# A new hand-written order for a fused cosine-attention and feed-forward kernel, with split first products

## The chip, the cores and the metric

The kernel runs on one core of one Trainium2 chip. The metric is the device time of one execution in microseconds (us): the median over several runs. Instruction times come from the hardware profiler's record of one execution. The engines are named as the profile names them: PE is the tensor engine, PEld its weight loads, DVE the vector engine, ACT the scalar engine, POOL the GpSimd engine and SP the engine that issues most transfers.

## The reference

Cosine attention over 8 batches of 12 heads (448 positions, 64 values each) feeds a feed-forward block with a hard-swish between its two matrices:

```python
q_n = q / (np.linalg.norm(q, axis=-1, keepdims=True) + 1e-06)
k_n = k / (np.linalg.norm(k, axis=-1, keepdims=True) + 1e-06)
scores = np.matmul(q_n, k_n.transpose(0, 1, 3, 2)) / tau
scores = scores - np.max(scores, axis=-1, keepdims=True)
attn = np.exp(scores)
attn = attn / (np.sum(attn, axis=-1, keepdims=True) + 1e-09)
attn_out = np.matmul(attn, v)
x = attn_out.transpose(0, 2, 1, 3).reshape(B * S, H * D)   # 3584 x 768
h = x @ w_in                                               # 768 x 2048
g = h * np.clip(h + 3.0, 0.0, 6.0) / 6.0
out = g @ w_out                                            # 2048 x 768
```

## The kernel before

**Work and tiling.** Heads are handled two at a time ("pairs"), one head in partitions 0 to 63 and the other in 64 to 127; there are 48 pairs, numbered 0 to 47, six to a batch. For each pair the kernel squares and sums q and k (SQ, RE), turns the sums into inverse norms (NO, four small ACT instructions), multiplies (NM), and transposes (on PE with TR for the first pairs and by a transfer, XD, later), copies the result to its place (CQ, CK, CS), multiplies keys by queries (SC), takes exponentials on ACT (EX), multiplies by the values (VA, after the values have been cast by VC), divides by the sums (FI), and turns the result around into xT (BK and CX on PE and DVE, or a transfer XB or XP).

**Feed-forward.** F.b.fc is one unit of the first product: six matmuls of 128x448 over the six 128-row parts of xT for batch b and column block fc, followed by an ACT instruction (FA) and a DVE instruction (FV) that write gT. The second product is done on pairs of 128-token tiles with seven products in place of eight (P.1 to P.7), which need sums and differences of halves of gT (G) and of w_out (WS). Their results are moved out and combined by PE.* steps on ACT or DVE, BO, RS and PL on POOL, then stored. The last two batches use the same scheme for the first product too (IS, XS, QA, QB, QC and what follows them).

**Half and whole rows.** A matmul reads 64 or 128 rows of the array. Scores of one head of a pair have an inner size of 64, so two matmuls, one on each half of the rows, run side by side; so do the values of the last, short group of keys (VA.i.3). All other matmuls use the whole 128 rows. The PE stream therefore alternates between half-row and whole-row stretches.

**Memory for results of PE.** At the start the scores go to two double banks, SC; the banks Y and Z hold transposes. OPEN closes the double banks and opens a ring of six single banks (M0, M1, Y, Z, M2, M3) that everything after it takes in turn. A bank can be taken again only when its reader is done. PV holds the values' products of one pair, so VA of the next pair waits for FI of this one.

**What sets the order.** PLAN is a hand-kept table of some 1,900 tokens. `run` performs them in turn; each token issues its instructions, and every engine executes its own in that order. A token's last letter says which engine does it, where there is a choice: v (DVE), a (ACT), p (POOL). The semaphores between engines are put in from the buffers that each instruction reads and writes. A token such as FA.0.2 or PE.3.1 performs a step that an earlier token has left behind with `post`. DP.n issues n products of zeros into an unused part of PV; their results are not read.

Of the kernel before, what the change touches and what calls it, by code (L numbers as in the profile page):

```python
# [120 lines left out]
def kernel(  # L121
# [15 lines left out]
    HP = H // 2  # L137
# [94 lines left out]
    def needs(*what):  # L232
        for w in what:
            assert w in issued or any(x < 0 for x in w[1:] if isinstance(x, int)), w
# [401 lines left out]
    def g_of(b):  # L636
        return gT[b % 2]
# [597 lines left out]
```

## Time and profile before

| | |
|---|---|
| median of 3 runs | 397.3 us (397.3 to 398.22) |
| the profiled execution | 397.24 us |
| its span, first to last instruction | 395.4 us |
| busy: PE, DVE, ACT, POOL | 97%, 78%, 75%, 75% of the span |
| products of zeros (DP) | 62 matmuls of 128x248 |

The span is 1.84 us shorter than the execution that it belongs to. [...]

### The profile page before, as it was taken

Reading aid. Unit: us, or ns where it says so; the run is one execution under the profiler, and the core shown is the slowest. Engines: PE = TensorE matmul, PEld = TensorE weight load, DVE = VectorE, ACT = ScalarE, POOL = GpSimd, SP = SyncE. Lnnn points to the kernel's source line nnn. Section 1 sums busy time; section 2 is a strip of 40 time slices with the busy share of each in tenths; the row PEclk is TensorE's granted clock in tenths of the full one; section 3 lists DMA queues with packets and bytes.
Section 4 is the critical chain, followed back from the end, with each engine's and each line's share of the span. In section 5 each row is a group of like instructions: output and inputs, shape, how many; then the busy total and the mean of one; then the engine's idle time right before and its main releaser. Section 6 shows DMA issues by size and latency. Waiting matters only on the chain.

```text
span 395.4 us, 10013 instructions
## 1 busy us (share of the span) xinstructions
PE 384.2 (97%) x3782; PEld 240.4 (61%) x3782; DVE 308.8 (78%) x545; ACT 295.3 (75%) x670; POOL 297.5 (75%) x269
## 2 busy tenths in 40 slices
PE   7898999999999999999999999999999999999995
PEld 5565556445655555655655556655566679977763
DVE  6998869988969697787767878853878968986862
ACT  6997999889966888887757876897787567744420
POOL 4999894899589947477848684778798988675752
PEclk9999999999999999999999999999999999999999
DMA  8989989798999797886995599665456350012124
GB/s 294 327 225 279 201 248 259 135 173 166 225 206 235 161 233 191 167 211 194 174 222 136 151 200 183 193 150 133 105 124 139 80 117 2 2 41 61 41 60 119
DMA packets 90239, 64.87 MB, mean 164 GB/s; under 512 B 55760, under 2 KB 89424, under 8 KB 90192
## 3 DMA queue, kind: packets, MB, share of 16 engines
q1 hardware_dynamic: 85280, 57.56, 59.1%
q0 software_dynamic: 4512, 6.29, 9.5%
q8 instruction: 29, 0.48, 0.5%
q10 hardware_dynamic: 400, 0.39, 0.3%
q14 instruction: 18, 0.15, 0.1%
HBM read 46.73 MB, written 11.01 MB: 146 GB/s over the span
## 4 chain that ended last, share of the span: by engine, by line
PE 87%; POOL 5%; DVE 2%; DMA 2%; issue 2%; ACT 1%; SPq 0%; POOLq 0%; DVEq 0%; ACTq 0%
PE M L671 18%; PE M L837 17%; PE PV L537 10%; PE V L837 6%; PE M L1026 6%; PE M L502 6%; PE Y L671 4%; PE Y L837 4%; PE Z L837 4%; PE Z L671 3%; POOL nrm L341 2%; PE Y L502 2%; PE Z L502 2%; POOL vx L363 1%; PE Y L1026 1%
## 5 line engine op out<-in xcount | busy, mean ns | idle before, releaser
L521 ACT ACTIVATE att<-M 128x448 bf16<-128x448 f32 x193 | 95.7, 561 | 13.9 <-PE M L502 12.2
L671 PE MATMUL M<-xT,w_in_sb 128*128 128x448 bf16 x396 | 82.9, 353 | 0.0
L671 PEld LDWEIGHTS <-w_in_sb 128*128 128x128 bf16 x576 | 53.1, 98 | 46.8 <-issue 3.4
L341 POOL TENSOR_TENSOR nrm<-big,r 128x896 bf16<-128x896 f32 (+1 forms) x36 | 61.7, 1720 | 15.0 <-ACT r L329 13.8
L537 PEld LDWEIGHTS <-att 128*128 128x128 bf16 (+1 forms) x1536 | 55.5, 97 | 23.0 <-issue 10.4
L537 PE MATMUL PV<-vx,att 128*128 128x65 bf16 (+1 forms) x1536 | 64.1, 193 | 0.5 <-POOL vx L363 0.5
L837 PEld LDWEIGHTS <-gT 128*128 128x128 bf16 x448 | 43.0, 98 | 27.7 <-issue 0.4
L686 DVE SCALAR_TENSOR_TENSOR gT<-u,M 128x448 bf16<-128x448 bf16 x66 | 39.5, 616 | 18.7 <-ACT u L680 18.4
L310 DVE TENSOR_REDUCE n<-big 128x14 f32<-128x896 f32 (+1 forms) x50 | 51.5, 1042 | 1.6 <-ACT big L296 1.3
L680 ACT ACTIVATE u<-M 128x448 bf16<-128x448 f32 x66 | 35.8, 555 | 10.8 <-PE M L671 9.7
L298 POOL TENSOR_TENSOR big<-big 128x896 f32<-128x896 f32 (+2 forms) x19 | 31.5, 1658 | 12.4 <-DMA big<-in_k_dram 6.9
L837 PE MATMUL M<-w_out_sb,gT 128*128 128x384 bf16 x224 | 40.4, 326 | 0.0
L837 PEld LDWEIGHTS <-gs 128*128 128x128 bf16 x296 | 28.1, 98 | 18.8 <-issue 1.3
L812 POOL TENSOR_TENSOR gT<-gT 128x1024 bf16<-128x1024 bf16 x15 | 31.9, 2125 | 9.5 <-DVE gs L812 9.0
L558 DVE TENSOR_TENSOR on<-PV,rc 128x512 bf16<-128x512 f32 x48 | 33.2, 691 | 1.6
L837 PE MATMUL M<-w_sum,gs 128*128 128x384 bf16 (+1 forms) x192 | 34.0, 323 | 0.0
L502 PE MATMUL M<-tT,kz 64*128 64x448 bf16 (+1 forms) x171 | 33.2, 354 | 0.6 <-DVE gT L686 0.4
L868 POOL TENSOR_TENSOR big<-big 128x384 f32<-128x384 f32 x14 | 18.3, 1308 | 17.7 <-ACT big L625 15.0
L812 POOL TENSOR_TENSOR gs<-gT 128x1024 bf16<-128x1024 bf16 x14 | 29.7, 2126 | 2.3 <-DVE gT L686 1.2
L521 ACT ACTIVATE att<-Z 128x448 bf16<-128x448 f32 x51 | 28.5, 559 | 1.3 <-PE M L502 1.0
L521 ACT ACTIVATE att<-Y 128x448 bf16<-128x448 f32 x50 | 28.0, 561 | 1.2 <-PE Z L502 1.2
L458 POOL COPY km<-tT 64x128 bf16<-64x128 bf16 x34 | 16.4, 483 | 12.5 <-PE Y L502 5.1
(146 smaller groups left out, 756.6 us busy)
## 6 DMA issues: line engine op xcount, KB each, us to landing
big<-in_q_dram SPq DMA_DIRECT2D x24, 448.0 KB, 4.4
big<-in_k_dram SPq DMA_DIRECT2D x24, 448.0 KB, 4.5
out_dram<-o SPq DMA_DIRECT2D x107, 96.0 KB, 2.2
big<-in_v_dram SPq DMA_DIRECT2D x68, 128.0 KB, 3.2
big<-in_v_dram SPq DMA_DIRECT2D x7, 448.0 KB, 7.6
w_out_sb<-in_moe_w_out_dram POOLq DMA_DIRECT2D x4, 768.0 KB, 10.2
w_in_sb<-in_moe_w_in_dram POOLq DMA_DIRECT2D x4, 384.0 KB, 5.8
w_in_sb<-in_moe_w_in_dram POOLq DMA_DIRECT2D x2, 768.0 KB, 8.3
```

The costliest lines, as they stand in the source:

```text
L298: engines[e].tensor_tensor(out=o, in0=i, in1=i, op=ALU.mult)
L310: nc.vector.tensor_reduce(out=n2s[d % 2][:, j % 2, c], in_=sq[:, :, :, :].rearrange("p g c d -> p (g c) d")[:, c, :], axis=AX.X, op=ALU.add,)
L341: engines[e].tensor_tensor(out=nrm[:, :, g, :].rearrange("p c g d -> p g c d"), in0=raw_of[j][:, g, :, :], in1=rs[d % 2][3][:, j % 2, :] . ...
L502: nc.tensor.matmul(o, ks, qt[rows], start=True, stop=True)
L521: nc.scalar.activation(out=o, in_=x, func=AF.Exp, scale=inv_tau)
L537: nc.tensor.matmul(pv_out(j, h), at[rows, n, q_cols(i // HP, j)], vt[rows, 3 + h if name == "M" else 5 * h + int(name[1]), :], start=(name ...
L558: nc.vector.tensor_tensor(out=on[:, :, :, :].rearrange("p j h d -> p h j d"), in0=pv4[:, :, :, 0:D], in1=rc[:, :, :].to_broadcast([128, 2, ...
L671: nc.tensor.matmul(ps[:, 0:S], w_in_sb[:, cc, fc * 128 : (fc + 1) * 128], x[:, cc, 0:S], start=(cc == 0), stop=(cc == CC - 1),)
L680: nc.scalar.activation(out=u[:, :], in_=ps[:, 0:S], func=AF.Relu, bias=0.5, scale=1.0 / 6.0)
L686: nc.vector.scalar_tensor_tensor(out=g[:, fc, c0 : c0 + S], in0=u[:, :], scalar=1.0, in1=ps[:, 0:S], op0=ALU.min, op1=ALU.mult,)
L812: engines[e].tensor_tensor(out=o[:, :, :], in0=x, in1=y, op=op)
L837: nc.tensor.matmul(m, lhs[:, c, :], rhs[:, c, c0 : c0 + width], start=(base is None and c == 0), stop=(c == KC - 1), skip_group_check=True,)
```

## The change

PLAN is replaced by another table for the same work. `mm1_unit` is split so that a unit of the first product may be begun before all six parts of xT are there: FP.b.fc.n takes a bank and does the first n parts, and F.b.fc does the rest into the same bank. The new table uses this for three units of batch 0 (FP.0.3.4, FP.0.1.4, FP.0.2.4). All other tokens are those of before, in another order, apart from these:

- Products of zeros: 33, 12, 4, 3, 4, 2, 1 and, ahead of VA.5.0, 3 (62 in all) become 28, 16, 3, 7, 3, 3 and 3 (63), all ahead of VA.0.0.
- The engine of many steps. NM: DVE 14 to 6, POOL 36 to 44. SQ from pair item 2 on, by DVE, ACT and POOL: 8, 21, 18 become 5, 22, 20. PE.2 to PE.5: ACT 44 to 33, DVE 12 to 23. G: POOL 30 to 29, DVE 40 to 41. XS: POOL 6 to 4, DVE 4 to 6. One half of IS.6 goes from POOL to DVE.

```diff
-    def mm1_unit(b, fc):
-        needs(*(("CX", i) for i in range(b * HP, (b + 1) * HP)))
+    part_of = {}
+
+    def mm1_chunks(b, fc, ps, chunks):
+        needs(*(("CX", b * HP + cc) for cc in chunks))
...
-        for cc in range(CC):
+        for cc in chunks:
...
+    def mm1_part(b, fc, n):
+        ps, key = bank_of(None, 1)
+        narrow.discard(key)
+        mm1_chunks(b, fc, ps, range(n))
+        part_of[(b, fc)] = ps, key, n
+
+    def mm1_unit(b, fc):
+        firsts_read.add((b, fc))
+        g, c0 = g_of(b), b % 2 * SR
+        if (b, fc) in part_of:
+            ps, key, n = part_of.pop((b, fc))
+        else:
+            (ps, key), n = bank_of(None, 1), 0
+            narrow.discard(key)
+        mm1_chunks(b, fc, ps, range(n, CC))
...
-    "SC.9.0 EX.9.0 F.0.4 RE.13 FI.7 SC.9.1 NM.11.p VC.10.p FA.0.4 FV.0.4 SC.9.2 TR.10 VA.8.0 VA.8.1 EX.9.1 NO.6 NM.13.p SC.9.3 CQ.11.v TR.11 CQ.10.v",
+    "VA.7.3 SC.9.0 SC.9.1 RE.12 EX.9.0 EX.9.1 NM.11.p CQ.11.v CQ.10.v FI.7 F.0.4 TR.11 CS.10.v FA.0.4 FV.0.4 SQ.14.p.0.7 SQ.13.p.0.7 SC.9.2 SC.9.3 CS.11.v",
```

**On PE, scores of pair 9.** L502 is a matmul of the scores; the two of a pair of rows run side by side on half rows. L671 (L669 in the changed kernel) is a unit of the first product on whole rows. Before, the first group of scores and the beginning of the unit F.0.4, and then the end of that unit and the second group:

```order
L502 LDWEIGHTS kz_81
L502 MATMUL M_652<-tT_84,kz_81 128x448
L502 LDWEIGHTS kz_81
L502 MATMUL M_653<-tT_84,kz_81 128x448
L671 LDWEIGHTS w_in_sb
L671 MATMUL Y<-xT_69,w_in_sb 128x448
```

```order
L671 LDWEIGHTS w_in_sb
L671 MATMUL Y<-xT_69,w_in_sb 128x448
L502 LDWEIGHTS kz_81
L502 MATMUL Z<-tT_84,kz_81 128x448
L502 LDWEIGHTS kz_81
L502 MATMUL M_654<-tT_84,kz_81 128x448
```

Now:

```order
L502 LDWEIGHTS kz_81
L502 MATMUL M_653<-tT_84,kz_81 128x448
L502 LDWEIGHTS kz_81
L502 MATMUL Y<-tT_84,kz_81 128x448
L502 LDWEIGHTS kz_81
L502 MATMUL Z<-tT_84,kz_81 128x448
L502 LDWEIGHTS kz_81
L502 MATMUL M_654<-tT_84,kz_81 128x448
L669 LDWEIGHTS w_in_sb
L669 MATMUL M_655<-xT_69,w_in_sb 128x448
```

The two groups of scores now stand side by side, and the unit behind them: two changes of row mode fewer at this place.

**On DVE, the end of pair 4.** L557 and L558 are FI, here of pairs 3 and 4; L310 is RE; the copies to tT are CQ, the one to kz_80 of 128x384 is CK.6, the others to kz are CS, those to xT CX. Before, from CX.2 to FI.4:

```order
L420 COPY xT_69<-Z 128x448
L310 TENSOR_REDUCE n_92<-big 128x14
L420 COPY tT_85<-Y 128x448 x2
L420 COPY kz_80<-Z 128x384
L420 COPY xT_69<-Y 128x448
L463 MEMSET kz_81 64x32
L420 COPY kz_81<-Z 64x64 x2
L557 RECIPROCAL rc<-PV 128x8
L558 TENSOR_TENSOR on<-PV,rc 128x2x4x64
```

Now, from CQ.6 to CK.6:

```order
L420 COPY tT_85<-Y 128x448 x2
L557 RECIPROCAL rc<-PV 128x8
L558 TENSOR_TENSOR on<-PV,rc 128x2x4x64
L310 TENSOR_REDUCE n_92<-big 128x14
L420 COPY xT_69<-Z 128x448
L420 COPY xT_69<-Y 128x448
L557 RECIPROCAL rc<-PV 128x8
L558 TENSOR_TENSOR on<-PV,rc 128x2x4x64
L420 COPY kz_80<-Z 128x384
```

FI.4, the second pair of L557 and L558, stood behind CK.6 and CS.7 and now stands ahead of them; FI.3 now stands behind the two copies to tT.

**On POOL, the end of the program.** L812 (L827) is G, L868 and L869 (L883, L884) are BO, L872 (L887) is RS. Before:

```order
L868 TENSOR_TENSOR big<-big 128x384
L869 TENSOR_TENSOR big<-big,o 128x384
L812 TENSOR_TENSOR gT_72<-gT_72 128x8x128
L868 TENSOR_TENSOR big<-big 128x384
L869 TENSOR_TENSOR big<-big,o 128x384
L872 TENSOR_TENSOR big<-big,o 128x384 x2
```

Now:

```order
L827 TENSOR_TENSOR big<-gT_72 128x1024
L883 TENSOR_TENSOR big<-big 128x384
L884 TENSOR_TENSOR big<-big,o 128x384
L883 TENSOR_TENSOR big<-big 128x384
L884 TENSOR_TENSOR big<-big,o 128x384
L827 TENSOR_TENSOR big<-gT_72 128x1024
L887 TENSOR_TENSOR big<-big,o 128x384 x2
```

G.1.12, the second L827, has come from DVE and stands between the last BO and the two RS.

More of the change, by code (lines that the diff above doesn't have):

```diff
@@ L660, in g_left @@
         left_done.add(b)
-    def mm1_unit(b, fc):
-        needs(*(("CX", i) for i in range(b * HP, (b + 1) * HP)))
+    part_of = {}
+    def mm1_chunks(b, fc, ps, chunks):
+        needs(*(("CX", b * HP + cc) for cc in chunks))
         assert all({2 * n, 2 * n + 1} <= weights_in for n, c in enumerate(FF) if c <= 128 * fc)
         assert not any(x in "34" for x, _ in in_summed)
-        firsts_read.add((b, fc))
-        x, g, c0 = xT[b % 2], g_of(b), b % 2 * SR
-        ps, key = bank_of(None, 1)
-        narrow.discard(key)
-        for cc in range(CC):
+        for cc in chunks:
             nc.tensor.matmul(
@@ L673, in mm1_unit @@
                 w_in_sb[:, cc, fc * 128 : (fc + 1) * 128],
-                x[:, cc, 0:S],
+                xT[b % 2][:, cc, 0:S],
                 start=(cc == 0),
@@ L1160 @@
         "GL": g_left, "WS": lambda x, *h: weight_sums(str(x), *((h[0] * KC // 2, KC // 2) if h else (0, KC))), "D": busy, "DP": busy_pv, "OPEN": open_ring,
-        "F": mm1_unit, "S": single_unit, "G": lambda x, n, e="v": g_sum(n, str(x), e), "P": product, "TB": tail_banks, "WR": wide_ring,
+        "F": mm1_unit, "FP": mm1_part, "S": single_unit, "G": lambda x, n, e="v": g_sum(n, str(x), e), "P": product, "TB": tail_banks, "WR": wide_ring,
         "IS": lambda x, e, *n: in_sum(str(x), e, *n), "XS": lambda b, x, *e: x_sum(b, str(x), *e), "QA": quad_first, "QB": quad_second, "QC": quad_third,
```

192 rows, old and new, of the table PLAN are left out of this document.

## The prediction

> **What bounds the kernel now.** I read the page first, then PE's time by stage, then PE's waits.
>
> ```profile
> span 395.4 us, 10013 instructions
> PE 384.2 (97%) x3782; PEld 240.4 (61%) x3782; DVE 308.8 (78%) x545; ACT 295.3 (75%) x670; POOL 297.5 (75%) x269
> PE 87%; POOL 5%; DVE 2%; DMA 2%; issue 2%; ACT 1%; SPq 0%; POOLq 0%; DVEq 0%; ACTq 0%
> ```
>
> PE is busy for 97% of the span and makes up 87% of the chain of waits. Where it is not busy, the windows tell (columns: stretch, its length, busy time and count on PE, PEld, DVE, ACT and POOL, then clock and transfers):
>
> ```profile
> 0.00:12.00 12.00, 9.40 (x67) 6.83 (x67) 8.11 (x20) 8.57 (x22) 6.59 (x21) 1.00 0.87 309
> 12.00:33.00 21.00, 18.33 (x276) 11.87 (x273) 19.78 (x39) 20.18 (x35) 20.34 (x22) 1.00 0.98 251
> 33.00:39.30 6.30, 5.18 (x96) 3.61 (x94) 5.26 (x15) 4.72 (x14) 6.29 (x4) 1.00 0.96 324
> 39.30:391.40 352.10, 351.28 (x3350) 218.10 (x3348) 275.11 (x473) 261.87 (x603) 264.31 (x224) 1.00 0.67 152
> ```
>
> From 39.3 us on PE is idle for 352.1 - 351.28 = 0.8 us: there the time is the sum of PE's issue distances. Before that it is idle for 6.4 us, and from 12 to 33 us ACT is busy for 20.18 of 21 us: the first 35 us or so are set by ACT with DVE and POOL close behind. So the change has two halves: what it takes from PE's own sum counts only behind the start, and at the start the other engines count.
>
> **Part 1: fewer changes of row mode.** One change is priced by PE's timeline (start, duration, instruction, tile, rows, count):
>
> ```profile
> 39.04 0.35 PE L502 MATMUL Y<-tT,kz 64*128 64x448 bf16 x1
> 39.32 1.31 PE L671 MATMUL M<-xT,w_in_sb 128*128 128x448 bf16 x6
> 40.47 0.35 PE L502 MATMUL M<-tT,kz 128*128 128x448 bf16 x1
> 40.66 1.30 PE L671 MATMUL M<-xT,w_in_sb 128*128 128x448 bf16 x6
> ...
> 22.20 0.41 PE L537 MATMUL PV<-vx,att 128*128 128x65 bf16 x8
> 22.54 0.36 PE L502 MATMUL SC<-tT,kz 64*128 64x448 bf16 x2
> ...
> 45.50 0.42 PE L537 MATMUL PV<-vx,att 128*128 128x65 bf16 x8
> 45.75 1.30 PE L671 MATMUL Y<-xT,w_in_sb 128*128 128x448 bf16 x6
> ```
>
> A whole-row matmul of 448 columns is followed 0.19 us later (40.47 to 40.66), a half-row one 0.28 us later where the next is whole (39.04 to 39.32): 0.09 us for the change. In the other direction eight value products take 0.34 us to a half-row successor (22.20 to 22.54) and 0.25 us to a whole one (45.50 to 45.75): again 0.09 us. I take 0.095, between the two-digit rows' bounds of 0.08 and 0.10.
>
> In the built orders I counted neighbours on PE of unlike row mode: 172 before, 146 now. All else on PE is the same, 3782 matmuls against 3783. Up to the first scores of pair 8, which started at 45.0 us, there are 49 changes before and 39 now; from there 123 and 107. The first ten lie where other engines set the time and are not credited; the other 16 x 0.095 give **-1.5 us**. Bounds: 26 x 0.10 = -2.6 if all count; 0 if waits take their place.
>
> [...]
>
> **Part 2: the start, to pair 8.** PE, ACT and DVE around the opening of the ring:
>
> ```profile
> 31.32 0.56 PE L398 MATMUL Z<-ident,nrm 128*128 128x128 bf16 x7 [0.32 <-POOL nrm L341]
> ...
> 34.13 0.48 PE L1142 MATMUL PV<-xT 128*128 128x248 bf16 x3 [1.12 <-DVE on L558]
> ...
> 35.02 0.36 PE L502 MATMUL M<-tT,kz 64*128 64x448 bf16 x2
> ```
>
> ```profile
> 23.42 8.60 ACT L521 ACTIVATE att<-SC 128x896 bf16<-128x896 f32 x11
> 32.51 0.54 ACT L521 ACTIVATE att<-SC 128x448 bf16<-128x448 f32 x1 [0.50 <-PE SC L499]
> ...
> 33.77 0.23 ACT L329 ACTIVATE r<-le 128x28 f32<-128x28 f32 x1
> 35.42 0.98 ACT L521 ACTIVATE att<-M 128x448 bf16<-128x448 f32 x2 [1.42 <-PE M L502]
> ```
>
> ```profile
> 30.40 0.68 DVE L420 COPY tT<-Y 128x448 bf16<-128x448 bf16 x2
> 31.92 0.36 DVE L420 COPY kz<-Z 128x384 bf16<-128x384 bf16 x1 [0.84 <-PE Z L398]
> 32.19 0.38 DVE L420 COPY xT<-Y 128x448 bf16<-128x448 bf16 x1
> ...
> 33.38 0.69 DVE L558 TENSOR_TENSOR on<-PV,rc 128x512 bf16<-128x512 f32 x1
> ```
>
> Read backwards: ACT stands still for 1.42 us because the ring's first scores come only at 35.02; PE waits 1.12 us for L558 (FI.4); and DVE came to it late, since it first waited 0.84 us for the transposes of pair 7 (PE at 31.32, itself late by POOL) and then did CK.6 and CS.7. In the new order FI.4 is ahead of CK.6: 0.84 of wait and about 0.9 of copies leave its way. Walking the new order by these durations, ACT goes straight from EX.5.3 to pair 6, and the ring's first scores come at about 34.0, a gain of 1.0 (by ACT's idle time at most 1.4).
>
> Not all is kept. DVE's steps listed between OPEN and pair 8 (four FV, two FI, two RE, a square, twelve copies; longest rows below) come to 11.5 us at the distances of the trace, where PE has 8.9 us of work; before, 9.0 against 9.65. The square there (SQ.10) has come from POOL and costs what the fourth row below says. Walked on, DVE frees the banks for pair 8 just before PE asks: about 44.3 against 45.0. 0.1 us of PE work has moved behind that point. The split units let PE do four sixths of a unit before the last copy to xT, which that walk includes. I take **-0.6 us**, with bounds -1.4 (ACT's gap closed) and +0.7 (the 11.5 us of DVE in full with 1 us of its own waits, 34.0 + 12.5 = 46.5, half of it reaching PE).
>
> ```profile
> L310 DVE TENSOR_REDUCE n<-big 128x14 f32<-128x896 f32 x46 | 49.1, 1079 | 1.0 <-ACT big L296 0.9
> L558 DVE TENSOR_TENSOR on<-PV,rc 128x512 bf16<-128x512 f32 x48 | 33.2, 691 | 1.6
> L686 DVE SCALAR_TENSOR_TENSOR gT<-u,M 128x448 bf16<-128x448 bf16 x66 | 39.5, 616 | 18.7 <-ACT u L680 18.4
> L298 DVE TENSOR_TENSOR big<-big 128x896 f32<-128x896 f32 x7 | 9.1, 1306 | 0.0
> L341 DVE TENSOR_TENSOR nrm<-big,r 128x896 bf16<-128x896 f32 x12 | 15.0, 1258 | 0.2 <-ACT r L329 0.2
> L341 POOL TENSOR_TENSOR nrm<-big,r 128x896 bf16<-128x896 f32 x34 | 59.9, 1766 | 12.3 <-ACT r L329 11.0 <-DMA tT<-nrm 0.5
> L812 POOL TENSOR_TENSOR gT<-gT 128x1024 bf16<-128x1024 bf16 x15 | 31.9, 2125 | 9.5 <-DVE gs L812 9.0
> L1142 PE MATMUL PV<-xT 128*128 128x248 bf16 x62 | 10.5, 329 | 3.9 <-DVE xT L1185 2.5 <-DVE on L558 1.4
> ```
>
> **Part 3: zeros.** 62 become 63, all where PE waits for others: 0. The three ahead of VA.5.0 go (about 0.3 us), counted in part 2. Uncovered, one costs about 0.1 us.
>
> **Part 4: new waits later.** Eight products move from DVE to POOL (1766 ns each, +14 us) and two squares; POOL gives up a sum, two XS and half of IS.6. In sum POOL gains some 10 us on 297.5, DVE loses some 6, ACT 4. By stretches of the table, the steps of DVE for pairs 12 to 15 come to 105% of PE's work there (26.4 against 25.2 us), those of POOL for pairs 36 to 39 to 106% (29.7 against 28.0); one more stretch of POOL, pairs 24 to 27, is at 100%; before, no stretch of four pairs was over 93% on these two engines. Much of it is not urgent, and the distances that matter to PE have not shrunk: from the last value product of a pair to the first of the next, the least PE work is 1.1 us now and 1.3 before, against 0.9 for FI. I take **+0.5 us**; bounds -0.8 (no wait at all behind 39.3) and +2.9 (both overhangs, 1.2 and 1.7, in full).
>
> **Part 5: the end.** Eight products take 1.3 us of PE:
>
> ```profile
> 384.64 1.46 PE L837 MATMUL V<-w_sum,big 128*128 128x384 bf16 x8
> 385.94 1.46 PE L837 MATMUL Y<-w_sum,gs 128*128 128x384 bf16 x8
> ```
>
> G.1.12 goes from DVE to POOL, behind both BO; its product comes four such groups, 5.2 us, after P.5.13, and the rest of BO (steps of 1.0) and G (2.1) need about 4.4: 0, bounds 0 and +1.
>
> Sum: 397.24 - 1.5 - 0.6 + 0.5 = 395.6 us, where the profiled execution stands 0.06 below the median, 397.3. **I predict 395.6 us.**
>
> **The rivals.**
>
> *POOL or DVE takes over (slower).* For pairs 36 to 39 POOL has 1.7 us more than PE; if its products there are late, the transfers that transpose them, and the scores behind them, stop PE. It decides once new waits exceed 2.1 us, and is slower beyond doubt at 3.3. DVE's overhang at 12 to 15 adds 1.2, the end 0.5: 397.24 - 2.1 + 3.4 = 398.5. For it: POOL is slowed while DVE reads two tiles, as here, where steps of about 1.0 take 2.4 us beside a long DVE sum:
>
> ```profile
> 310.91 2.42 POOL L868 TENSOR_TENSOR big<-big 128x384 f32<-128x384 f32 x1 [0.68 <-ACT big L625]
> 313.40 2.39 POOL L869 TENSOR_TENSOR big<-big,o 128x384 f32<-128x384 f32 x1
> 315.87 1.00 POOL L872 TENSOR_TENSOR big<-big,o 128x384 f32<-128x384 f32 x1
> ```
>
> [...] Against the rival: PE lost 0.8 us in 352 with POOL at 75%. Chance 0.17.
>
> *No change to speak of.* DVE's 11.5 us eat the gain of the start, and waits of about 1 us the rest: 397.24 - 1.5 + 1.0 = 396.7. For it: the one long wait behind 39.3 us is already a DVE one, at 45.0. Chance 0.23.
>
> ```profile
> PE M L502 <- DVE gT L686: 0.4, 1, 0.4
> ```
>
> *All of it counts.* The start closes ACT's whole gap and all 26 changes are on the path: 397.24 - 2.5 - 1.4 = 393.4. Against it: ten of the changes lie where PE waits anyway. Chance 0.10.
>
> **How the numbers follow.** My forecast has 0.50. A difference under 0.3% (1.2 us) cannot be told from none by a measurement of this kernel; that is 396.1 to 398.5. Faster: 0.47 of the forecast's 0.50 and the third rival, 0.57. Same: the second rival, 0.03 of the forecast and a little of the first, 0.28. Slower: 0.15. The range, 393.6 to 398.6, leaves out the third rival's lower half and the first's upper half; the forecast's own is 394.6 to 396.5.
>
> **What would show it.** Part 1: half-to-whole distances unchanged, PE busy down by about 2 us with 3783 matmuls. Part 2: ACT's gap of 1.42 gone, the ring's first scores near 34.0, those of pair 8 near 44.3, the wait of L1142 for L558 gone. Part 4: PE idle behind 39.3 us under 1.5 us, POOL busy near 307. Wrong would be: PE waits for POOL's products (through transfers) or DVE's FI of a microsecond or more between pairs 12 and 40, or the scores of pair 8 no earlier than 45.0.

## The result, and the profile after

The changed kernel took 395.14 us (median of 5 runs, 395.05 to 396.15) beside 397.6 us of the kernel before (5 runs on the same chip, 397.3 to 398.22): a ratio of 0.9934, with a 95% interval from 0.9915 to 0.9952. The forecast was 395.6 us. Each kernel's runs form a tight group at its lowest times and a looser one 1 to 4 us above it, so "lowest" below is the lowest run, and kernels are compared by it and by spans. The lowest was 2.25 us lower, the span 2.4.

The page of the changed kernel (span; busy time, share and count of each engine; shares of the chain of waits):

```profile
span 393.0 us, 10013 instructions
PE 381.5 (97%) x3783; PEld 241.1 (61%) x3783; DVE 303.0 (77%) x548; ACT 291.8 (74%) x658; POOL 300.6 (76%) x278
PE 89%; ACT 4%; POOL 2%; DVE 2%; DMA 1%; issue 1%; DVEq 0%; ACTq 0%; POOLq 0%
```

Its windows, cut as those of before (length, then busy time and count on PE, PEld, DVE, ACT, POOL):

```profile
0.00:12.00 12.00, 8.01 (x62) 5.99 (x63) 7.77 (x19) 7.88 (x20) 7.59 (x23) 1.00 0.87 306
12.00:33.00 21.00, 18.71 (x279) 11.96 (x280) 20.46 (x37) 20.12 (x38) 20.31 (x20) 1.00 1.08 289
33.00:39.30 6.30, 5.90 (x96) 3.92 (x94) 5.99 (x18) 6.09 (x14) 6.12 (x7) 1.00 0.85 248
39.30:389.00 349.70, 348.91 (x3353) 219.22 (x3350) 268.22 (x476) 257.74 (x590) 266.53 (x231) 1.00 0.68 152
```

Behind 39.3 us PE idles for 0.79 us, as before (0.82). From 33 to 39.3 us it idles for 0.4 us instead of 1.1. The waits of PE behind 39.3 us are these two (total, times, longest):

```profile
PE Z L1041 <- DVE Z L1117: 0.5, 1, 0.5
PE M L502 <- DVE gT L701: 0.2, 1, 0.2
```

The place that the prediction's second part spoke of, the opening of the ring, in the timeline of all engines:

```profile
32.44 0.69 DVE L558 TENSOR_TENSOR on<-PV,rc 128x512 bf16<-128x512 f32 x1
...
32.96 1.33 ACT L521 ACTIVATE att<-SC 128x896 bf16<-128x896 f32 x2
...
33.17 0.36 DVE L420 COPY kz<-Z 128x384 bf16<-128x384 bf16 x1
...
33.91 0.37 PE L502 MATMUL M<-tT,kz 64*128 64x448 bf16 x2
...
34.29 0.98 ACT L521 ACTIVATE att<-M 128x448 bf16<-128x448 f32 x2
```

L558 is now done ahead of CK.6, the ring's first scores start at 33.91 (forecast 34.0, before 35.02), and ACT goes from the last double bank at 32.96 into the ring at 34.29 without the gap of 1.42.

To see where the time came from, I compared the start of the same matmul in both traces, corrected by the PE work, at its usual distances, that one order had done by then and the other had not (products of zeros left out). The changed kernel's gain by place:

| first scores of pair | 6 | 8 | 16 | 24 | 32 | 40 | end of attention | last QC | span |
|---|---|---|---|---|---|---|---|---|---|
| gain, us | 1.11 | 1.16 | 1.80 | 2.43 | 2.70 | 2.96 | 3.01 | 2.35 | 2.4 |

So 1.2 comes from the start, and it grows to 3.0 as the row changes are left out; 0.65 is lost again at one place near 368 us, at the wait for L1117 above. The start alone differs by some 0.1 us from one profiled execution to the next: with the same table up to there, pair 8's scores start at 43.85 us in the changed kernel and at 43.72 to 43.79 in five of the runs below.

### The profile page after: what moved, and what is told of

It reads as the page before. It is cut to its first block, busy times and chain, and to the rows that moved or that the text cites. A ratio compares the mean times of both kernels' runs of the same rounds, so it can differ in the third digit from the quotient of the medians.

```text
span 393.0 us, 10013 instructions
## 1 busy us (share of the span) xinstructions
PE 381.5 (97%) x3783; PEld 241.1 (61%) x3783; DVE 303.0 (77%) x548; ACT 291.8 (74%) x658; POOL 300.6 (76%) x278
## 4 chain that ended last, share of the span: by engine, by line
PE 89%; ACT 4%; POOL 2%; DVE 2%; DMA 1%; issue 1%; DVEq 0%; ACTq 0%; POOLq 0%
PE M L852 19%; PE M L669 18%; PE PV L537 10%; PE M L502 6%; PE V L852 6%; PE M L1041 6%; PE Y L669 6%; PE Z L669 4%; PE Y L852 3%; PE Z L852 3%; PE Z L502 2%; ACT att L521 2%; PE Z L1041 1%; PE Y L502 1%; PE Y L1041 1%; DMA big<-in_q_dram 1%
## 5 line engine op out<-in xcount | busy, mean ns | idle before, releaser
L341 POOL TENSOR_TENSOR nrm<-big,r 128x896 bf16<-128x896 f32 (+1 forms) x44 | 73.7, 1682 | 15.2 <-ACT r L329 13.3
L669 PEld LDWEIGHTS <-w_in_sb 128*128 128x128 bf16 x576 | 53.7, 98 | 47.9 <-issue 2.9
L669 PE MATMUL M<-xT,w_in_sb 128*128 128x448 bf16 x378 | 78.1, 353 | 0.0
L310 DVE TENSOR_REDUCE n<-big 128x14 f32<-128x896 f32 (+1 forms) x50 | 51.0, 1041 | 3.6 <-ACT big L296 2.7
L701 DVE SCALAR_TENSOR_TENSOR gT<-u,M 128x448 bf16<-128x448 bf16 x63 | 37.8, 617 | 18.7 <-ACT u L695 18.4
L695 ACT ACTIVATE u<-M 128x448 bf16<-128x448 f32 x63 | 34.3, 559 | 14.4 <-PE M L669 13.8
L852 PE MATMUL M<-w_out_sb,gT 128*128 128x384 bf16 x248 | 44.9, 326 | 0.0
L298 POOL TENSOR_TENSOR big<-big 128x896 f32<-128x896 f32 (+4 forms) x23 | 35.6, 1550 | 7.5 <-DVE n L310 5.8
L852 PE MATMUL M<-w_sum,gs 128*128 128x384 bf16 (+1 forms) x216 | 38.4, 323 | 0.0
L502 PE MATMUL M<-tT,kz 64*128 64x448 bf16 x172 | 34.5, 354 | 0.3 <-DVE gT L701 0.2
L558 DVE TENSOR_TENSOR on<-PV,rc 128x512 bf16<-128x512 f32 x48 | 33.2, 692 | 1.7
L827 POOL TENSOR_TENSOR gs<-gT 128x1024 bf16<-128x1024 bf16 x13 | 28.0, 2156 | 5.2 <-PE Z L852 5.1
L458 POOL COPY km<-tT 64x128 bf16<-64x128 bf16 x34 | 12.9, 380 | 19.1 <-PE Y L502 10.2
L827 POOL TENSOR_TENSOR gT<-gT 128x1024 bf16<-128x1024 bf16 x10 | 22.6, 2260 | 5.8 <-ACT o L625 3.9
L669 PE MATMUL Y<-xT,w_in_sb 128*128 128x448 bf16 x114 | 24.7, 352 | 0.0
```

Of the source, the lines that this page charges most:

```text
L298: engines[e].tensor_tensor(out=o, in0=i, in1=i, op=ALU.mult)
L310: nc.vector.tensor_reduce(out=n2s[d % 2][:, j % 2, c], in_=sq[:, :, :, :].rearrange("p g c d -> p (g c) d")[:, c, :], axis=AX.X, op=ALU.add,)
L341: engines[e].tensor_tensor(out=nrm[:, :, g, :].rearrange("p c g d -> p g c d"), in0=raw_of[j][:, g, :, :], in1=rs[d % 2][3][:, j % 2, :] . ...
L502: nc.tensor.matmul(o, ks, qt[rows], start=True, stop=True)
L558: nc.vector.tensor_tensor(out=on[:, :, :, :].rearrange("p j h d -> p h j d"), in0=pv4[:, :, :, 0:D], in1=rc[:, :, :].to_broadcast([128, 2, ...
L669: nc.tensor.matmul(ps[:, 0:S], w_in_sb[:, cc, fc * 128 : (fc + 1) * 128], xT[b % 2][:, cc, 0:S], start=(cc == 0), stop=(cc == CC - 1),)
```

## The experiments

### The two halves of the order, each alone

PLAN is cut at SC.8.0, the first scores of pair 8. One run takes the new table up to there and the old one behind it, the other the reverse. Steps that the two tables have on different sides of the cut are moved or left out once, none of them on PE: LQ.13, LQ.14, SQ.12 and SQ.13 stand ahead of it in the first run, W.4, FV.0.3 and VC.9 in the second.

```diff
 PLAN, new start and old rest
-the tokens of before, up to SC.8.0
+the tokens of the change, up to SC.8.0
 the tokens of before, from SC.8.0
```

> The changed order up to the first scores of pair 8, then the old order for what is left: 162 changes of row mode, 39 + 123. Theory (start and later stages are independent, the start is worth the 1.0 us by which pair 8's scores come earlier in the changed kernel, less 0.1 us of work moved behind them): span 394.4, 1.0 below the kernel before; PE idle behind 39.3 us stays near 0.8. Rival (the gain of the start is given back later, because DVE or POOL arrive late at pair 8): span 395.2 to 395.6, with new waits of PE between 44 and 60 us.

Measured: lowest 396.85 against 397.19, ratio 0.9979 (0.9955 to 1.0003), span 394.9. The gain was 1.27 at pair 8, 0.66 at pair 9 and 0.5 at the end. Behind the cut, PE waits for L558 once more:

```profile
44.84 0.42 PE L537 MATMUL PV<-vx,att 128*128 128x65 bf16 x8 [0.54 <-DVE on L558]
```

So the theory that the start and what follows are independent fails here: the start's gain is real, and more than half of it is lost at this seam. It is not the old order as such that loses it: the run with one place alone, below, has the old order behind pair 8 and keeps its 1.0.

> The old order up to the first scores of pair 8, then the changed order for what is left: 156 changes, 49 + 107. Theory (16 changes at 0.095 us, waits between pairs 8 and 47 a little fewer, and the changed kernel's one wait of 0.7 us near 368 us kept): span 394.1 to 394.4, 1.0 to 1.3 below the kernel before. Rival (the gain is all in the later order, and the start only shifts it): span 393.0 to 393.3, as the changed kernel.

Measured: lowest 396.13, ratio 0.9968 (0.9942 to 0.9994). Between pair 8 and the end of attention it gains 1.85 us, and the last 25 us take 0.67 back. Its profiled execution (span 396.3) was disturbed at the start, which belongs under the last heading. The first run's 1.27 and this 1.85 add up to 3.1, where the whole change has 3.01 at that place: the two halves account for it.

### One place of the start alone

```diff
 PLAN of the kernel before
-"... EX.5.2 NM.7.p TR.7.Z CK.6.v ... BK.3.Y CX.3.v ... CS.7.v EX.5.3 NO.4 BK.1.Y FI.4 ..."
+"... EX.5.2 NM.7.p BK.3.Y CX.3.v TR.7.Z BK.1.Y FI.4 CK.6.v ... CS.7.v EX.5.3 NO.4 ..."
```

> The kernel before with one place changed: the division of pair 4 (FI.4), with the turn-around products ahead of it, stands before the copies of pair 6's keys on DVE. Theory (this one place is the start's gain): ACT's gap of 1.42 us at 34 us and PE's wait of 1.12 us go, the ring's first scores come 1.0 to 1.7 us earlier, and the span falls by 0.7 to 1.2, to 394.2 to 394.7. Rival (DVE is full from there to pair 8, so that the place alone only moves the wait to the bank reuse near 44 us): span 395.0 to 395.5.

Measured: span 394.4, lowest 396.15, ratio 0.9952 (0.993 to 0.9975). The gain is 0.98 at pair 8 and 1.01 at the end. Its window:

```profile
33.00:39.30 6.30, 6.30 (x100) 4.03 (x100) 5.66 (x17) 6.05 (x17) 6.29 (x4) 1.00 0.93 285
```

PE is busy for all 6.30 us, where before it was for 5.18. Moving the division of pair 4, with the turn-around steps BK.3, CX.3 and BK.1, ahead of the copies, with nothing else of the change, is worth 1.0 of the start's 1.2 us, and the old order behind it keeps that to the end. Together with the second half's net gain (1.85 less 0.67) it makes 2.2 of the 2.4 us.

### The price of a change of row mode

```diff
 PLAN of the changed kernel, at 16 pairs; here pair 35
-"... SC.35.1 EX.35.1 SC.35.2 CK.37.v G.1.6.p G.6.6.p XP.32 VA.34.1 P.3.6 ..."
+"... SC.35.1 EX.35.1 VA.34.1 SC.35.2 CK.37.v G.1.6.p G.6.6.p XP.32 P.3.6 ..."
```

> The changed kernel with 32 changes of row mode put back: for 16 pairs between 18 and 46 one group of whole-row value products of the pair before stands ahead of the third scores instead of right behind them (0.23 us of PE work moved, nothing else). 178 changes against 146. Theory (a change costs PE 0.095 us wherever PE is the bound): 32 x 0.095 = 3.0 us longer, span 396.0, PE's idle time behind 39.3 us unchanged at about 0.8. Rival (a change hides under the matmuls around it, and the 1.5 us came from fewer waits): span 393.0 to 393.5. [...]

Measured: lowest 398.40, 3.35 above the changed kernel's 395.05, so 0.105 for each of 32 changes; ratio to before 1.0027 (1.0007 to 1.0047). Between the first scores of pair 16 and the end of attention, where all the moves lie, its trace falls 3.31 us behind that of the changed kernel. The profiled execution's span, 398.6, holds 2.3 us more, from its first 18 us, which the change of the table doesn't touch. PE at pair 35 in the changed kernel:

```profile
233.32 0.35 PE L502 MATMUL M<-tT,kz 64*128 64x448 bf16 x1
...
233.53 0.36 PE L502 MATMUL M<-tT,kz 64*128 64x448 bf16 x1
233.82 0.42 PE L537 MATMUL PV<-vx,att 128*128 128x65 bf16 x8
234.08 0.65 PE L852 MATMUL M<-w_out_sb,gT 128*128 128x384 bf16 x3
```

and with the value products in between, with the window behind the start:

```profile
237.73 0.35 PE L502 MATMUL M<-tT,kz 64*128 64x448 bf16 x1
...
238.01 0.42 PE L537 MATMUL PV<-vx,att 128*128 128x65 bf16 x8
238.37 0.36 PE L502 MATMUL Z<-tT,kz 64*128 64x448 bf16 x1
...
238.66 0.34 PE L852 MATMUL M<-w_out_sb,gT 128*128 128x384 bf16 x1
```

```profile
39.30:394.00 354.70, 353.90 (x3383) 222.13 (x3380) 270.76 (x480) 259.85 (x595) 269.11 (x233) 1.00 0.68 151
```

Joined, the two pairs of scores follow each other after 0.21 us, where one is recorded with 0.35: they overlap, and the distances from start to start are compared here. Parted, PE goes from half to whole rows after 0.28, and from whole to half after 0.36 instead of the 0.26 that eight value products take to a whole-row successor. From the first of these rows to the output product it is 0.76 us joined (233.32 to 234.08) and 0.93 parted (237.73 to 238.66): 0.17 for two changes. PE's idle time stays at 0.80, so the 3.3 us are the changes themselves and no waits. The prediction's 0.095 was a little low: the 0.103 to 0.105 found here lie just above its upper bound of 0.10.

### The engine of eight products

```diff
 PLAN of the changed kernel, likewise NM.20, 24, 26, 31, 38, 39 and 40
-"... NM.17.p ..."
+"... NM.17.v ..."
```

> The changed kernel with the eight normalising products (L341) that had gone from DVE to POOL put back on DVE, at their places; all else is the changed kernel. POOL about 14 us less busy, DVE about 10 more. Theory (neither engine sets the time behind the start): span 393.0 within 0.4. Rival one (POOL's load costs waits that fewer products there would end): up to 0.5 faster, PE idle behind 39.3 us under 0.5. Rival two (DVE is the tighter of the two, 105% of PE's work at pairs 12 to 15, and was relieved by the change): slower by 0.5 or more, with PE waiting for DVE steps between pairs 12 and 40.

Measured: span 401.0, lowest 402.78, ratio to before 1.0148 (1.0113 to 1.0182): 8 us more than the changed kernel for eight steps of 1.26 us. The losses begin behind pair 14's scores. Its window there, and two waits of PE in it:

```profile
84.00:95.00 11.00, 9.30 (x98) 4.94 (x98) 10.93 (x14) 9.06 (x24) 4.61 (x4) 1.00 0.68 166
```

```profile
85.89 1.30 PE L669 MATMUL Y<-xT,w_in_sb 128*128 128x448 bf16 x6 [0.94 <-DVE gT L701]
91.48 0.35 PE L502 MATMUL Y<-tT,kz 64*128 64x448 bf16 x1 [0.69 <-DVE gT L701]
```

and the same stretch in the changed kernel:

```profile
84.00:92.60 8.60, 8.60 (x99) 4.61 (x96) 8.45 (x13) 8.38 (x22) 3.88 (x4) 1.00 0.92 239
```

DVE is busy for 8.45 of 8.60 us even in the changed kernel, ACT for 8.38 and POOL for 3.88. One more product on DVE makes the gates (L701) late, and the gates free the ring's banks. DVE is the tight engine here, as the second rival said: the move of products to POOL is not a load on the change but what lets its order run.

```diff
 PLAN of the kernel before, the same eight
-"... NM.17.v ..."
+"... NM.17.p ..."
```

> The kernel before with the eight normalising products (L341) of the change on POOL instead of DVE, at their old places; all else is the kernel before. Putting them back on DVE had made the changed kernel 8 us longer. Theory (the engine of a step and the order belong together; the old order gave DVE the room where its products stood, and POOL's products there come late for the transfers that transpose them): 0 to 3 us longer than before, span 395.4 to 398.5, with PE waiting for nrm, tT or scores behind POOL. Rival (moving the products to POOL is a gain by itself): 0.4 us or more shorter, span 395.0 or less, PE's idle time behind 39.3 us under 0.5.

Measured: lowest 401.06, 3.8 above the kernel before beside it (397.26), ratio 1.0077 (1.0047 to 1.0107). The size is a little over the theory's 0 to 3. (Its profiled execution, span 400.9, has a disturbed start of some 1.4 us besides.) It loses 4.0 us between pairs 16 and 24. The window there, and the longest waits of PE in it:

```profile
95.00:165.00 70.00, 66.55 (x644) 38.13 (x643) 51.48 (x82) 54.31 (x125) 53.79 (x44) 1.00 0.85 201
```

```profile
100.79 0.35 PE L502 MATMUL M<-tT,km 128*128 128x448 bf16 x1 [1.07 <-DVE gT L686]
144.91 0.37 PE L502 MATMUL M<-tT,kz 64*128 64x448 bf16 x2 [1.26 <-DVE o L864]
```

In the old order the same steps on POOL hold PE up for 3.45 of 70 us. For the second of these waits the profile shows how: DVE itself waits until 143.66 us for a sum on POOL, and comes to L864 only then.

```profile
DVE gT L812 <- POOL gs L812: 3.6, 1, 3.6
```

The chain behind the first wait was not followed to POOL. The assignment is neither good nor bad by itself; order and engine belong together.

### The wait of 0.51 us in the tail

PE and what leads to its wait at 368 us in the changed kernel:

```profile
365.57 1.04 POOL L659 COPY gT<-gT 128x1024 bf16<-128x1024 bf16 x1 [2.81 <-ACT u L1081]
366.57 0.66 POOL L1067 TENSOR_TENSOR att<-att 128x224 f32<-128x224 f32 x1
367.30 0.66 POOL L1068 TENSOR_TENSOR att<-att 128x224 f32<-128x224 f32 x1
```

```profile
368.00 0.63 DVE L1117 TENSOR_TENSOR Z<-att,M 128x448 f32<-128x448 f32 x1 [0.27 <-POOL att L1068]
```

```profile
368.68 0.75 PE L1041 MATMUL Z<-att,big 128*128 128x224 bf16 x6 [0.51 <-DVE Z L1117]
```

POOL's sums of QD.7.7 stand behind its copy of GL.6, which waits 2.81 us for ACT. The experiment puts them ahead of it.

```diff
 PLAN of the changed kernel
-"... QC.7.5 GL.6.p QD.7.7 RS.11 ... P.7.10 PE.7.10.v QR.7.7 QC.7.6 ..."
+"... QC.7.5 QD.7.7 GL.6.p RS.11 ... QB.7.7 QR.7.7 ... P.7.10 PE.7.10.v QC.7.6 ..."
```

> The changed kernel with one place near the end changed: on POOL the sum of the last unit (QD.7.7) stands ahead of the copy of the left-over columns (GL.6), and on DVE the step that reads it (QR.7.7) right behind its products. Theory (PE's wait of 0.5 to 0.7 us at 368 us comes from POOL standing behind that copy): the wait goes and the span falls by 0.5 to 0.7 us, to 392.3 to 392.5. Rival (the next step, the copy itself or the activation behind it, is late instead): span 392.8 to 393.2.

Measured: span 392.9, lowest 395.01 against the changed kernel's 395.05; ratio to before 0.9922 (0.9896 to 0.9948). The wait is gone and the gain at the last QC is 3.09 us, but PE then loses 0.48 us two groups later, because DVE comes to L879, which frees a bank, only behind a sum:

```profile
369.19 0.69 DVE L827 TENSOR_TENSOR gs<-gT 128x1024 bf16<-128x1024 bf16 x1
369.80 0.55 DVE L879 TENSOR_TENSOR o<-V,big 128x384 f32<-128x384 f32 x1
```

```profile
370.40 1.46 PE L852 MATMUL V<-w_out_sb,gT 128*128 128x384 bf16 x8 [0.20 <-DVE o L879]
```

(Eight matmuls from 368.62 would end at 369.92; the next eight start at 370.40.) So three runs reorder DVE there, each on top of this one.

```diff
 first: the bank's release ahead of the sum
-"... QV.7.6.2 P.6.11 G.6.13.v PE.6.11.v QC.7.7 ..."
+"... QV.7.6.2 P.6.11 PE.6.11.v G.6.13.v QC.7.7 ..."
```

> The run with the late sum early, and also the copy with addition that frees a bank (L879 of product 6 of pair 11) ahead of a sum of 128x1024 (L827, product 6 of pair 13) on DVE. In that run DVE came to L879 at 369.80 us, behind the sum of 0.69 us, and PE lost 0.48 us for it (8 matmuls from 368.62 and the next 8 only at 370.40 instead of 369.92). Theory (that one wait held the gain of the late sum): span 392.4 to 392.5, 0.5 to 0.6 below the changed kernel. Rival (the transfers out or POOL set the end, and the loss moves on once more): span 392.8 to 393.0.

Measured: span 394.1, lowest 395.94, ratio 0.9977 (0.9959 to 0.9994): worse by about 1 us. DVE and POOL:

```profile
369.80 2.42 DVE L827 TENSOR_TENSOR gs<-gT 128x1024 bf16<-128x1024 bf16 x1
```

```profile
369.56 2.12 POOL L827 TENSOR_TENSOR big<-gT 128x1024 bf16<-128x1024 bf16 x1 [1.80 <-DVE gT L1095]
```

Started 0.24 us behind POOL's sum, DVE's took 2.42 us in place of 0.69; POOL's ended at 371.68, and DVE's ends 0.54 later. PE then waited 0.63 and 0.38 us.

```diff
 second: the gates behind the release, the sum still right behind the gates
-"... QV.7.6.2 P.6.11 G.6.13.v PE.6.11.v QC.7.7 ..."
+"... P.6.11 PE.6.11.v QV.7.6.2 G.6.13.v QC.7.7 ..."
```

> The run with the late sum early, with DVE's two gates (L1095) of the second scale behind, not ahead of, the copy with addition that frees a bank (L879 of product 6 of pair 11). The sum of 128x1024 (L827) stays right behind the gates, so that it and POOL's sum of the same size, which waits for the same gates, still start together, both some 0.5 us later. Theory (with the first attempt at the end, DVE's sum started 0.24 us behind POOL's and took 2.42 us instead of 0.69; started first it is done before POOL slows it): the sum takes 0.7, the wait of 0.48 us at 370.4 is gone, span 392.4 to 392.6. Rival (any start beside POOL's sum is slowed; the 0.69 was luck of 0.1 us): the sum takes 2 us or more, PE waits 0.6 us or more at 372 to 378, span 393.5 to 394.

Measured: span 393.4, lowest 395.48, ratio 0.994 (0.9917 to 0.9963). The sum took 0.69, as the theory said, and the wait at 370.4 went; but the gates are now late themselves, and with sums still slowed later (the next two, from 370.92 us, took 2.50 us, where the first attempt needed 1.29 for two with POOL idle) PE lost 0.41 and 0.31 us in two new waits:

```profile
369.62 2.29 PE L852 MATMUL V<-w_out_sb,gT 128*128 128x384 bf16 x13 [0.41 <-DVE gT L1095]
```

```diff
 third: as the first, and POOL's sum moved to DVE
-"... G.7.13.v G.1.13.v G.7.12.v G.6.12.p G.2.12.v ..."
+"... G.7.13.v G.1.13.v G.7.12.v G.6.12.v G.2.12.v ..."
```

> The first attempt at both waits of the end, with the sum of 128x1024 (L827, product 6 of pair 12) that POOL had done there on DVE, at its place in the order. POOL then does nothing from 367.8 to 376 us. Theory (DVE's sum took 2.42 us there only because POOL read the same kind of tile beside it; alone it takes 0.69): every L827 on DVE behind 366 us takes 0.6 to 0.7 us, the waits of 0.63 and 0.38 us at 372 to 378 are gone, and the wait of 0.48 us for L879 too: span 392.4 to 392.6. Rival (DVE's chain from the last gates to the last products has no room for one step more, 0.6 us): sums of 0.7 us, but PE still waits 0.3 us or more for L827 or L1095, span 392.8 to 393.2.

Measured: lowest 394.57, ratio 0.9909 (0.9879 to 0.9939). With POOL idle, the same sum at the same place:

```profile
370.98 0.68 DVE L827 TENSOR_TENSOR gs<-gT 128x1024 bf16<-128x1024 bf16 x1
```

```profile
378.31 1.47 PE L852 MATMUL V<-w_out_sb,gT 128*128 128x384 bf16 x8 [0.17 <-DVE gT L827]
```

0.68 us in place of 2.42: POOL's sum was the cause. But PE still lost about 0.34 us at 378.3 (the eight before start at 376.67 and take 1.30), and from the first output product behind the last QC to the last eight it needed 18.68 us (370.06 to 388.74), against 18.82 with the late sum early alone (368.62 to 387.44). So the rival is partly right too: behind 366 us DVE's chain from the last gates to the last sums has no room (from 369.45 to 378.7 us no gap between its steps is listed), and what is taken from one wait turns up in the next. (This execution's span, 394.2, has 1.4 us from a late start; PE waits 1.4 us for POOL's L341 there.) Its ratio is the best of all runs, but the interval overlaps the changed kernel's, and on different chips the two are not told apart.

### Fewer changes still

```diff
 PLAN, with the second tail above; six places, among them pair 30
-"... VA.29.1 ... SC.30.0 ... EX.30.0 F.3.11 FA.3.11 ... VA.29.3 FI.29 RE.36 SC.30.1 SC.30.2 ..."
+"... VA.29.1 ... F.3.11 SC.30.0 ... EX.30.0 FA.3.11 ... VA.29.3 FI.29 RE.36 SC.30.1 SC.30.2 ..."
```

> The late sum early, the next run's cure of the end, and six places between pairs 8 and 30 where groups of half-row scores now stand together: 134 changes of row mode instead of 146. Theory: 12 x 0.10 = 1.2 us, and 0.5 at the end against the run with the late sum early: span 391.2. The chain from first scores to the bank's next use gets no longer at two of the six places (unit moved ahead of the group), while at four the scores come earlier or later than the search put them. Rival (the search kept the groups apart because ACT, busy nearly all the time at pairs 8 to 17, or DVE there, would be late): new PE waits of 0.3 us or more at pairs 8, 14, 16 or 17 that eat the gain, span 392 to 393.

Measured: span 405.2, lowest 406.37, ratio 1.0225 (1.0198 to 1.0252). Against the changed kernel it lost 12 us where 1.2 us of changes were saved, many times more than the rival said. It is 2.9 us behind at the first scores of pair 14, 8.2 at pair 24 and 11.7 at pair 32; only one of the six places was followed up. At pair 30 (windows, then PE, then DVE):

```profile
204.10:207.50 3.40, 1.74 (x18) 0.64 (x18) 1.45 (x4) 2.29 (x5) 3.10 (x6) 1.00 1.15 263
207.50:211.00 3.50, 3.50 (x13) 1.62 (x11) 2.44 (x4) 2.15 (x4) 1.94 (x3) 0.51 1.37 135
```

```profile
206.69 0.35 PE L502 MATMUL M<-tT,kz 64*128 64x448 bf16 x1 [1.66 <-DVE gT L701]
...
208.60 3.96 PE L852 MATMUL M<-w_sum,gs 128*128 128x384 bf16 x16
```

```profile
206.01 0.62 DVE L701 SCALAR_TENSOR_TENSOR gT<-u,M 128x448 bf16<-128x448 bf16 x1 [2.07 <-ACT u L695]
```

The unit F.3.11 now stands ahead of the three groups of scores, which take the next six banks. The ring has six, so the last is the unit's own, free only when the unit's gate (L701) has read it, behind ACT, at 206.6. PE waits 1.66 us, and the clock then falls to half (0.51) for 3.4 us: 16 matmuls take 3.96 us, where 8 take 1.30 at full rate. In the changed kernel the last score takes the bank of the first, which the exponentials have read by then: at this place the ring of six is the reason to keep the groups apart.

### No products of zeros

```diff
 PLAN of the changed kernel, likewise DP.16, 3, 7, 3, 3 and 3
-"... SQ.3.a.0.7 DP.28 TR.0.Z ..."
+"... SQ.3.a.0.7 TR.0.Z ..."
```

> The changed kernel without its 63 products of zeros; all else is the same, and the output too. 138 changes of row mode instead of 146, the eight all in the start. Theory (the zeros stand where PE waits anyway and cost or bring nothing): span 393.0 within 0.4. Rival (they keep PE's clock up: with them the matmuls come at half the rate only until about 6 us; without them the half rate begins with the first transposes at 8.5 us and lasts some 3.6 to 5.4 us, so that up to 3 us of real work takes twice as long): 1 to 3 us longer by the first scores of pair 6, and about as much at the end. Rival three (eight changes fewer and no zeros ahead of the scores): up to 0.7 us shorter.

Measured: span 393.9, lowest 395.71, ratio to before 0.9967 (0.9945 to 0.999). So without the zeros the kernel is 0.9 us longer by span and 0.66 by the lowest run. PE's transposes in it:

```profile
8.44 0.93 PE L398 MATMUL Z<-ident,nrm 128*128 128x128 bf16 x7 [8.44 <-DVE nrm L341]
...
16.69 0.95 PE L398 MATMUL Z<-ident,nrm 128*128 128x128 bf16 x7
...
23.10 0.55 PE L398 MATMUL Y<-ident,nrm 128*128 128x128 bf16 x7
```

Seven transposes take 0.93 us until past 17 and 0.55 at 23. By the clock records the half rate lasts until 21 us, where with the zeros it ends at 6.1. From 8.4 to 21 us POOL is busy for 11.68 of the 12.6 us and PE for 9.48, so other engines set the time there, and 12.6 us at half rate cost only 0.9: less than the clock rival's 1 to 3, and not nothing.

## Why the prediction was right, and where its steps were not

The forecast was off by 0.5 us and right in direction. Its parts against what the traces and runs show:

| part | forecast | measured | from |
|---|---|---|---|
| 1, row changes | -1.5 | -1.65 | 16 x 0.103, the run with changes added (3.31 / 32) |
| 2, start | -0.6 | -1.2 | gain at pair 8; 1.0 of it in the run with one place alone |
| 3, zeros | 0 | 0 | not separated; 62 against 63 |
| 4, later waits | +0.5 | -0.2 | what is left of the gain to the end of attention, 3.01, less the two above |
| 5, end | 0 | +0.65 | gain 3.01 falls to 2.35 |
| sum | -1.6 | -2.4 | span -2.4; lowest run -2.25 |

*Part 1* was right in mechanism and nearly in size. Added changes cost 0.103 to 0.105 us each with no wait; the bounds of 0.08 and 0.10 were too narrow, since four starts rounded to 0.01 leave 0.07 to 0.11. The ten changes of the start earned at most 0.2: of the 1.16 up to pair 8 the one place has 0.98.

*Part 2* named the right place, the division of pair 4 ahead of CK.6, and the ring's first scores came at 33.91 where it said 34.0. It was mis-sized behind that: it took DVE's 11.5 us of steps up to pair 8 as eating 0.4 of the 1.0, and no such wait appeared; pair 8's scores started at 43.85 where it said 44.3. No PE work has moved behind that point either: both traces have as many matmuls of each shape ahead of it, but for one product of zeros more. And the row from 12 to 33 us has POOL busy for 20.34 us, ACT for 20.18: ACT is not ahead of POOL there, as the prediction's first reading had it. One sentence was wrong: split units give PE nothing early, since each FP in the new table stands directly ahead of its own F, so the four and the two matmuls follow each other as in an unsplit unit.

*Part 3* called the zeros free because PE waits there. Whether one more or less is free was not separated; as a whole they are worth 0.9 us, by the clock and not by PE's time.

*Part 4* had the wrong sign. It charged DVE's 105% at pairs 12 to 15 and POOL's 106% at 36 to 39. Of the first, a wait of 0.19 us for a gate (L701) at pair 12 (67.07 us) is all that showed, of the second nothing. The -0.2 is a remainder and has no run of its own. POOL was busy for 300.6 us, not near 307, in part since its steps became shorter:

```profile
L341 POOL TENSOR_TENSOR nrm<-big,r 128x896 bf16<-128x896 f32 x42 | 71.9, 1718 | 12.8 <-ACT r L329 10.9 <-DMA tT<-nrm 0.9 <-issue 0.4
L458 POOL COPY km<-tT 64x128 bf16<-64x128 bf16 x34 | 12.9, 380 | 19.1 <-PE Y L502 10.2 <-PE M L502 4.8 <-PE Z L502 3.2
```

(L341 took 1766 ns in the row quoted before, and L458 483 ns.) The view behind it was right all the same: DVE at pairs 12 to 15 is at its limit, as the run with products back on DVE shows, which loses 2.2 us between the scores of pairs 14 and 16 and 7.6 by pair 40.

*Part 5* looked at G.1.12 and found 0; that step costs nothing, since PE has no wait behind 368.7 us. It missed the order of POOL's copy and sums at 365 us. What is shown is that this order makes the wait, and that ending it brings little, since DVE is full behind it.

Too little was credited at the start and for the later waits (1.3 us together) and a loss at the end was missed (0.65); about half cancelled, so that the total came this close is partly luck. The first rival's place was real, but as a limit that the order keeps to, not as a cost of the change. The second rival's eaten start did not come, and of the third only the closed gap of the start did, not the pay for all 26 changes.

## What to carry to other kernels

Where one engine is busy all the time, count what each neighbour costs it: a change between half and whole rows is 0.10 us here, and it adds up. Before joining groups or moving a step to another engine, walk who frees the buffer that the next group takes: six joints that saved 1.2 us cost 12, and eight steps moved back cost 8. When a wait near the end is removed, look at once at which engine is then busy without a gap; if it is the one you leaned on, the gain stays there.

## What the hardware showed that was not expected

**A wait can cost twice.** In the run with the old start and new rest, two windows of the profiled execution:

```profile
31.70:35.10 3.40, 1.76 (x22) 1.27 (x21) 2.35 (x10) 2.42 (x7) 3.21 (x5) 1.00 1.06 226
35.10:38.50 3.40, 3.40 (x45) 2.36 (x42) 1.80 (x6) 1.40 (x3) 3.40 (x4) 0.51 0.95 345
```

and the same place in the kernel before, undisturbed in its profiled execution:

```profile
32.00:35.40 3.40, 2.07 (x37) 1.55 (x35) 3.06 (x12) 1.35 (x6) 3.32 (x3) 1.00 0.92 255
```

With PE busy for 1.76 of 3.4 us the granted clock was half for the next 3.4 us; with 2.07 it was not. By the clock records, its changes in the first of these runs come at 7.88, 35.19 and 38.60 us, whole multiples of 3.41 us apart, and the windows above are cut close to these times. The clock fell in the same way, to 0.50 or 0.51 in the stretch that follows, behind 1.74 us in the run with 134 changes (above), behind 1.75 in the run with the eight products on POOL (31.0 to 34.4 us), and behind 1.33 in the run with the changes added (10.4 to 13.8). Where the limit lies is not shown: in the run with the eight products on POOL, a stretch of this length with 1.67 us (143.66 to 147.07) did not bring the clock down (1.00 from 95 to 165 us). Of the three profiled executions with the old start, two met this at 34 to 35 us (this run and the one with the eight products on POOL) and the kernel before did not; pair 8's scores came 2.1 and 1.5 us later in them than in the kernel before. The waits at 32 to 35 us are those that the change takes away, so the kernel before may meet this in some of its other executions; that was not shown.

**Of two sums side by side, the later one was slowed.** A 128x1024 sum on DVE took 0.69 us alone or started first, and 2.42 us when POOL's like sum had begun 0.24 us earlier: it ended 0.54 us behind POOL's end. The other way round, POOL's sum took 2.56 us in place of 2.12 when DVE's had begun 0.11 us earlier (the run with the late sum early, 369.30 and 369.19).
